# Thirteen wider chunks for fourteen equal ones in the two mixers of a fused attention and mixer kernel

## The chip, the core and the metric

The kernel runs on one core of one Trainium2 chip. The time is device microseconds from launch to end, the median of three runs. TensorE (PE in the rows) multiplies, VectorE (DVE) and ScalarE (ACT) do the elementwise work, GpSimd (POOL) and SyncE (SP) issue most of the transfers.

## The reference

Three blocks follow each other on two samples of 3136 tokens with 256 features: attention whose weights are a squared ReLU, a mixer with a low-rank mix along the tokens, and a mixer with a Fourier transform along tokens and features. Both mixers end in the same feed-forward pair of matmuls with 1024 hidden features.

```python
scores = (1 / S) * z @ z.T
a = u * (np.maximum(scores, 0) ** 2 @ v)             # attention, gated by u

u1 = a + (a.T @ U @ V).T                             # mixer 1: U is 3136x32, V is 32x3136
x = u1 + np.maximum(u1 @ w_ch1, 0) @ w_ch2

u2 = x + np.real(fft(fft(x, axis=1), axis=2))        # mixer 2
un = (u2 - mean(u2)) / np.sqrt(var(u2) + 1e-6)       # over the features
out = u2 + np.maximum(un @ w2_ch1, 0) @ w2_ch2
```

## The kernel before, in words

Everything is kept transposed: features on the 128 partitions (two halves), tokens along the free axis. Each fp32 operand of a large matmul is split into a high part rounded to float32r and a low rest, and a product is made of three float32r matmuls: high by high, high by low, low by high.

The attention runs first, in 14 blocks of 448 queries (7 for each sample). For every pair of key blocks ScalarE makes ReLU and square in a tile of the rotation P (`ptile`, four buffers of 896 columns), VectorE casts it into h and subtracts into l (three buffers each), and TensorE uses h and l two visits later (`LAG = 2`).

The mixers are two layers of 14 chunks of 448 tokens (`CH`), 7 for each sample, none across the border between the samples. One loop (line 1163 on) runs over steps `i`, eight for each chunk, 224 in all. A step issues `hidden(k)` of the present chunk: six matmuls of 448 columns into psH (lines 378 to 380), then ScalarE's ReLU into Hh (line 383) and VectorE's rest into Hl (line 384). Then it issues `project` of the hidden block of two steps before: six matmuls of 448 columns into psC (lines 403 to 405). So Hl of a step has two steps to become ready. In layer 2 the last projection of a chunk is put ahead of the next chunk's first `hidden`, and `finish` follows it at once: two multiplications by rs (line 425), two additions (line 427), two stores.

The order is written out by hand: instructions stand on their engines as the loop issues them, each engine takes its own in that order, and semaphores only hold it back. Beside the two matmul blocks a step advances generators in a list `active`, each to its next `yield`:

- `prep1` (layer 1): a chunk's token mix, two matmuls Gs by Vs of 448 columns (line 268), an addition into x (a P tile), the split into h and l. `Vs` has one buffer and is loaded on GpSimd's queue (line 254).
- `prep2` (layer 2): a chunk's mean and variance, over a row that goes through DRAM (mu, rs) and comes back broadcast; rs has two buffers.
- `fourier(b)`: the transform along 64 and the feature transform of one sample, in 28 advances. `starts` has it begin at step 65 for the first sample and at step 122 for the second. It has to end before the first chunk of layer 2 of its sample is prepared, which the loop asserts.

The list `calm` holds the two `fourier` generators: at a chunk's first step (`k == 0`) they are passed over, so they advance in seven steps of eight. The tables `events`, `folds` and `behind` place the other Fourier pieces (`halves49`: folding, the transform along 49) at given steps. xT is a tile for each sample, 3136 columns wide in each feature half; layer 1 writes its result back into it.

Of the kernel before, what the change touches and what calls it, by code (L numbers as in the profile page):

```python
# [21 lines left out]
CH = 448  # L22
NC = S // CH
NP = 13
# [55 lines left out]
def program(ctx, tc, zT, v, uT, U, V, w1a, w2a, w1b, w2b, b49, f64, fd, rep, mask, out):  # L80
# [25 lines left out]
    def c2(t):  # L106
        return t.rearrange("p (a n) -> p a n", a=2)
# [9 lines left out]
    rs_d = dram.tile([NB * NC, CH], F32, tag="rsd", name="rsd")  # L117
    mu_d = dram.tile([NB * NC, CH], F32, tag="mud", name="mud")
# [38 lines left out]
    def words(raw, np_, n):  # L157
# [5 lines left out]
        e = raw[0:np_, 4 * n : 4 * n + n // 2].bitcast(U16)  # L163
# [82 lines left out]
    class Chunk:  # L246
        def __init__(self, layer, b, c):
            self.layer, self.b, self.c = layer, b, c
            self.sl = slice(c * CH, c * CH + CH)

        def load(self):
            self.vs = com.tile([128, CH + 48], F32R, tag="Vs", name="Vs", bufs=1)[:, 0:CH]
            for k in (0, 64):
                late_dma(out=self.vs[k : k + 64, :], in_=V_d[:, self.sl])
# [4 lines left out]
        def prep1(self):  # L259
            b, vs = self.b, self.vs  # L260
            a = late["xT"][b][:, :, self.sl]
            yield
            if self.c or self.b:
                yield
            x, h, l = c2(ptile()), c2(ctile("h", F32R)), c2(ctile("l", F32R))
            for k in range(2):
                ps = misc()
                mm(ps[:, 0:CH], Gs[b][:, k * 128 : k * 128 + 128], vs, start=True, stop=True)  # L268
                tt(out=x[:, k], in0=ps[:, 0:CH], in1=a[:, k], op=ALU.add)
                hcopy(h[:, k], x[:, k])  # L270
                sub(l[:, k], x[:, k], f(h[:, k]))
                yield
            self.x, self.h, self.l = x, h, l

        def small(self, k):
            if self is not chunks[-1]:
                return late["small"](F32R if k == 2 else F32)
# [4 lines left out]
        def turned(self, s):  # L282
# [3 lines left out]
            q = late["mp"].tile([128, 16], F32, tag="vq", name="vq")[:, 0:14]  # L286
# [3 lines left out]
        def gathered(self, q):  # L290

            vv = late["mp"].tile([32, 64], F32, tag="vv", name="vv")[:, 0:56].rearrange("p (j i) -> p j i", i=4)
# [4 lines left out]
        def spread(self, row_d):  # L297
# [3 lines left out]
            late_dma(out=row_d.rearrange("(p j) -> p j", j=32), in_=turn_back[0:14])  # L301

        def prep2(self):
            b, mp = self.b, late["mp"]
# [3 lines left out]
            pad = late["pad"][:, 0:14]  # L308
            x = late["xT"][b][:, :, self.sl]
            last = self is chunks[-1]  # L310
            nr = b * NC + self.c
# [9 lines left out]
            mu = self.small(2) if last else mp.tile([128, CH], F32, tag="mu", name="mu", bufs=1)  # L321
            late_dma(out=mu, in_=mu_d[nr].partition_broadcast(128))
            for _ in range(1 if last else 3):
                yield
            cc = f(mp.tile([128, 2, CH], F32R, tag="Th", name="Th", bufs=1)) if last else c2(ptile())
            sq = c2(ptile())
# [16 lines left out]
            var, y, r0, ve = (mp.tile([32, 16], F32, tag=t, name=t)[:, 0:14] for t in ("va", "vy", "vr", "ve"))  # L343
# [12 lines left out]
            self.rs = mp.tile([128, CH], F32, tag="rs", name="rs")  # L356
            late_dma(out=self.rs, in_=rs_d[nr].partition_broadcast(128))
# [9 lines left out]
        def split(self, x, y):  # L367
            self.x, self.h, self.l = x, c2(ctile("h", F32R)), c2(ctile("l", F32R))
# [4 lines left out]
        def hidden(self, k):  # L373
            w, mp = late["w"][self.layer][0], late["mp"]
            ps = late["psH"].tile([128, 512], F32, tag="H", name="psH")
# [5 lines left out]
            h = mp.tile([128, CH], F32R, tag="Hh", name="Hh", bufs=3)  # L381
            l = mp.tile([128, CH], F32R, tag="Hl", name="Hl", bufs=3)
            act(out=h, in_=ps[:, 0:CH], func=AF.Relu)  # L383
            stt(out=l, in0=ps[:, 0:CH], scalar=0.0, in1=f(h), op0=ALU.max, op1=ALU.subtract)  # L384
# [3 lines left out]
        def project(self, k):  # L388
# [11 lines left out]
            for a, k, h, l in parts:  # L400
                wh, wl = w.last(k, 0, a), w.last(k, 1, a)
                dst = self.acc[a][:, 0:CH]
# [6 lines left out]
        def finish(self):  # L409
            b = self.b  # L410
            if self.layer == 1:
                for a in range(2):
                    tt(out=late["xT"][b][:, a, self.sl], in0=self.acc[a][:, 0:CH], in1=self.x[:, a], op=ALU.add)
            else:
                o = c2(ptile())
                if self is chunks[-1]:
                    t0, n = self.c * CH, CH // 2
                    for cuts in (((0, 0, CH),), ((1, 0, n), (1, n, CH))):
                        for a, s, e in cuts:
                            tt(out=o[:, a, s:e], in0=self.acc[a][:, s:e], in1=self.x[:, a, s:e], op=ALU.add)  # L420
                            store = nc.scalar.dma_start if a and s == 0 else load
                            store(out=out[b, a * 128 : a * 128 + 128, t0 + s : t0 + e], in_=o[:, a, s:e])
                    return
                for a in range(2):
                    tt(out=o[:, a], in0=self.acc[a][:, 0:CH], in1=self.rs, op=ALU.mult)
                for a in range(2):
                    tt(out=o[:, a], in0=o[:, a], in1=self.x[:, a], op=ALU.add)
                    load(out=out[b, a * 128 : a * 128 + 128, self.sl], in_=o[:, a])

    chunks = [Chunk(y, b, c) for y in (1, 2) for b in range(NB) for c in range(NC)]  # L430


    def attention(stack):
# [83 lines left out]
        def stage():  # L517
            return att.tile([128, 1152], I32, tag="stg", name="stg")
# [730 lines left out]
```

## Time and profile before

| | |
|---|---|
| time, median of 3 runs | 1113.71 us (1113.55 to 1113.74) |
| the profiled execution's own time | 1114.02 us |
| its span, first to last instruction | 1112.2 us |
| attention, until the first step of the mixers | 528.8 us |
| 224 steps of the mixers | 528.8 to 1108.2 us |
| TensorE's granted clock | 1.00 of full speed throughout |
| busy share of PE, DVE, ACT | 100%, 76%, 57% |

Between the span and the execution's own time lie 1.8 us, before the first and after the last instruction. A matmul's recorded duration is its passage through the array, and consecutive matmuls overlap; what one costs TensorE is the distance from its start to the next one's start, which the timeline shows. A line of the timeline that ends in x2 or more stands for so many neighbours, its duration from the first one's start to the last one's end.

### The profile page before, as it was taken

The page shows a single profiled execution, that of the slowest core. Times are in us where ns is not written, and L with a number is a line of the kernel's source. Part 1 is how long each engine was busy: PE and PEld are TensorE (multiplying, and loading weights), DVE is VectorE, ACT ScalarE, POOL GpSimd, SP SyncE. Part 2 cuts the span into 40 slices and gives each one's busy share as a digit, 9 for nine tenths or more (in the row PEclk, how much of TensorE's full clock was granted, in tenths as well). Part 3 has the DMA queues.
Part 4 walks back from the last instruction along what each step waited for, and adds up shares of the span by engine and source line. Part 5 has one row for each costly group of instructions (what it writes and reads, how often), then busy time and mean ns, then how long its engine had stood idle before and what let it go on. Part 6 is the DMA issues. An engine that isn't in the chain of part 4 may idle for free.

```text
span 1112.2 us, 21470 instructions
## 1 busy us (share of the span) xinstructions
PE 1107.0 (100%) x8282; PEld 1060.2 (95%) x8282; DVE 846.5 (76%) x1598; ACT 636.3 (57%) x1101; POOL 189.0 (17%) x313
## 2 busy tenths in 40 slices
PE   9999999999999999999999999999999999999998
PEld 8999999999999999999989999999999999999997
DVE  8877887888788876676667778577678898778863
ACT  8777777878787776675333444343345444435431
POOL 2202221221122102202211112110132111011110
PEclk9999999999999999999999999999999999999999
DMA  5222222424222234211823445331145322121110
GB/s 168 78 57 62 66 77 69 121 72 129 56 71 60 70 100 121 51 34 34 263 70 92 124 153 141 83 78 45 36 98 145 78 66 61 41 59 50 57 44 34
DMA packets 87815, 92.16 MB, mean 83 GB/s; under 512 B 27622, under 2 KB 76506, under 8 KB 87712
## 3 DMA queue, kind: packets, MB, share of 16 engines
q1 hardware_dynamic: 70544, 58.90, 17.8%
q0 software_dynamic: 16816, 31.68, 12.2%
q8 instruction: 65, 1.06, 0.4%
q14 instruction: 38, 0.31, 0.1%
q10 hardware_dynamic: 352, 0.21, 0.1%
HBM read 60.87 MB, written 29.85 MB: 82 GB/s over the span
## 4 chain that ended last, share of the span: by engine, by line
PE 99%; ACT 0%; DMA 0%; DVE 0%; issue 0%; SPq 0%; DVEq 0%; ACTq 0%
PE psO L628 37%; PE psS L586 9%; PE psH L378 8%; PE psC L405 8%; PE psH L380 8%; PE psC L403 8%; PE psH L379 8%; PE psC L404 8%; PE ps_m L1009 0%; DMA zraw<-in_zT 0%; PE ps_g L1009 0%; PE ps_x L1009 0%; PE psS L233 0%; PE ps_g L233 0%; PE ps_x L268 0%; PE ps_m L971 0%
## 5 line engine op out<-in xcount | busy, mean ns | idle before, releaser
L628 PE MATMUL psO<-h,Vt 64*128 64x448 f32 x2744 | 324.0, 359 | 0.2 <-DVE h L597 0.2
L628 PEld LDWEIGHTS psO<-h,Vt 64*128 64x128 f32 x2744 | 280.8, 184 | 3.4 <-DVE h L597 0.9
L383 ACT ACTIVATE Hh<-psH 128x448 fp32r<-128x448 f32 x224 | 121.5, 543 | 241.8 <-PE psH L380 238.6
L93 DVE TENSOR_TENSOR l<-P,h 128x896 fp32r<-128x896 f32 (+2 forms) x237 | 224.8, 954 | 35.4 <-ACT h L90 18.2
L384 DVE SCALAR_TENSOR_TENSOR Hl<-psH,Hh 128x448 fp32r<-128x448 f32 x224 | 138.1, 619 | 107.6 <-ACT Hh L383 105.5
L602 ACT ACTIVATE P<-psS 128x896 f32<-128x896 f32 (+1 forms) x181 | 160.4, 886 | 76.6 <-PE psS L586 74.9
L628 PE MATMUL psO<-l,Vt 64*128 64x448 f32 x1372 | 185.6, 359 | 0.0
L603 ACT ACTIVATE P<-P 128x896 f32<-128x896 f32 (+1 forms) x181 | 167.4, 925 | 5.7
L604 DVE CAST h<-P 128x896 fp32r<-128x896 f32 (+1 forms) x181 | 110.6, 611 | 74.7 <-ACT P L603 73.3
L378 PE MATMUL psH<-h,w 128*128 128x448 f32 x448 | 165.0, 368 | 0.0
L380 PE MATMUL psH<-h,w 128*128 128x448 f32 x448 | 162.4, 362 | 0.0
L405 PE MATMUL psC<-Hh,w 128*128 128x448 f32 x448 | 162.3, 362 | 0.0
L379 PE MATMUL psH<-l,w 128*128 128x448 f32 x448 | 162.2, 362 | 0.0
L404 PE MATMUL psC<-Hl,w 128*128 128x448 f32 x448 | 162.1, 362 | 0.0
L403 PE MATMUL psC<-Hh,w 128*128 128x448 f32 x448 | 162.0, 362 | 0.0
L628 PEld LDWEIGHTS psO<-l,Vt 64*128 64x128 f32 x1372 | 145.6, 184 | 1.1
L586 PE MATMUL psS<-Q,KT 64*128 64x448 f32 x1002 | 132.3, 360 | 0.0
L586 PEld LDWEIGHTS psS<-Q,KT 64*128 64x128 f32 x1002 | 104.1, 184 | 1.7 <-issue 0.4
L378 PEld LDWEIGHTS psH<-h,w 128*128 128x128 f32 x448 | 84.1, 188 | 6.3 <-ACT P L90 0.3
L379 PEld LDWEIGHTS psH<-l,w 128*128 128x128 f32 x448 | 84.2, 188 | 5.8
L404 PEld LDWEIGHTS psC<-Hl,w 128*128 128x128 f32 x448 | 84.0, 187 | 6.0
L403 PEld LDWEIGHTS psC<-Hh,w 128*128 128x128 f32 x448 | 83.9, 187 | 5.7 <-issue 0.2
(287 smaller groups left out, 1149.4 us busy)
## 6 DMA issues: line engine op xcount, KB each, us to landing
out<-P SPq DMA_DIRECT2D x27, 224.0 KB, 1.9
uT<-in_uT SPq DMA_DIRECT2D x13, 448.0 KB, 3.8
aTd<-aT POOLq DMA_DIRECT2D x13, 448.0 KB, 3.0
aNd<-aT POOLq DMA_DIRECT2D x104, 56.0 KB, 2.2
vraw<-in_v SPq DMA_DIRECT2D x18, 256.0 KB, 4.4
scr<-wst SPq DMA_DIRECT2D x16, 256.0 KB, 2.0
Vs<-Vd POOLq DMA_DIRECT2D x28, 112.0 KB, 2.6
xT<-aTd SPq DMA_DIRECT2D x7, 448.0 KB, 4.8
```

The costliest lines, as they stand in the source:

```text
L93: tt(out=o, in0=a, in1=b, op=ALU.subtract)
L378: mm(ps[:, 0:CH], wh, self.h[:, a], start=a == 0, stop=False)
L379: mm(ps[:, 0:CH], wh, self.l[:, a], start=False, stop=False)
L380: mm(ps[:, 0:CH], wl, self.h[:, a], start=False, stop=a == 1)
L384: stt(out=l, in0=ps[:, 0:CH], scalar=0.0, in1=f(h), op0=ALU.max, op1=ALU.subtract)
L403: mm(dst, wh, h, start=k == 0, stop=False)
L404: mm(dst, wh, l, start=False, stop=False)
L405: mm(dst, wl, h, start=False, stop=k == 7)
L586: mm(dst[:, 0:w], k, q[r, kq, o : o + w], start=(kk, kq) == (0, 0), stop=kk == 1)
L602: act(out=A[:, x].rearrange("p (a n) -> p a n", a=2), in_=ps[:, :, 0:w], func=AF.Relu, scale=1.0 / S)
L603: act(out=A[:, x], in_=A[:, x], func=AF.Square)
L628: mm(o[fa][i][:, 0:CH], vt[r, j, k, fa * 128 : fa * 128 + 128], x[r, j * CH : j * CH + CH], start=p == 0 and fa not in [t[1][0] for t in t ...
```

## The change

Both layers take 13 chunks: layer 1 has widths 448, four times 496, eight times 480; layer 2 has twice 512, ten times 480, 448. The seventh chunk of each layer lies across the border between the samples. The loop has 208 steps. A chunk's `parts` lists which of its columns belong to which sample. In layer 1 the border chunk's token mix takes two matmuls in place of one (224 and 256 columns, each with its sample's Gs) and four loads of Vs in place of two; in layer 2 its stores are cut in two.

Wider tiles take more room, so P has three buffers in place of four, rs one in place of two, the conversion scratch `stg` 1024 columns in place of 1152 (the exponent field is kept in the lowest 16 bits of the words themselves), and the last gate of the attention takes its two tiles from h and l in place of P. The two samples' xT become one tile X.

The list `calm` goes, so both `fourier` generators advance in every step. The second starts at step 114 in place of 122, and the `halves49` events are placed at written-out steps.

```diff
+CW = 512
+WIDTHS = {1: [CH] + 4 * [496] + 8 * [480], 2: 2 * [CW] + 10 * [480] + [CH]}
+L1 = len(WIDTHS[1])
...
     def ctile(tag, dt=F32, **k):
-        return com.tile([128, 2 * CH], dt, tag=tag, name=tag, **k)
+        return com.tile([128, 2 * CW], dt, tag=tag, name=tag, **k)
     def ptile():
-        return ctile("P", bufs=4)
+        return ctile("P", bufs=3)
...
     class Chunk:
-        def __init__(self, layer, b, c):
-            self.layer, self.b, self.c = layer, b, c
-            self.sl = slice(c * CH, c * CH + CH)
+        def __init__(self, layer, c):
+            self.layer, self.c, self.n = layer, c, WIDTHS[layer][c]
+            t0 = sum(WIDTHS[layer][:c])
+            t1 = t0 + self.n
+            self.sl = slice(t0, t1)
+            self.parts = [
+                (b, slice(max(t0, b * S) - t0, min(t1, b * S + S) - t0), slice(max(t0, b * S) - b * S, min(t1, b * S + S) - b * S))
+                for b in range(NB)
+                if t0 < b * S + S and t1 > b * S
+            ]
...
             for k in (0, 64):
-                late_dma(out=self.vs[k : k + 64, :], in_=V_d[:, self.sl])
+                for _, here, there in self.parts:
+                    late_dma(out=self.vs[k : k + 64, here], in_=V_d[:, there])
...
                 ps = misc()
-                mm(ps[:, 0:CH], Gs[b][:, k * 128 : k * 128 + 128], vs, start=True, stop=True)
-                tt(out=x[:, k], in0=ps[:, 0:CH], in1=a[:, k], op=ALU.add)
+                for b, here, _ in self.parts:
+                    mm(ps[:, here], Gs[b][:, k * 128 : k * 128 + 128], vs[:, here], start=True, stop=True)
+                tt(out=x[:, k], in0=ps[:, 0:n], in1=a[:, k], op=ALU.add)
...
-            self.rs = mp.tile([128, CH], F32, tag="rs", name="rs")
-            late_dma(out=self.rs, in_=rs_d[nr].partition_broadcast(128))
+            self.rs = mp.tile([128, CW], F32, tag="rs", name="rs", bufs=1)[:, 0:n]
+            late_dma(out=self.rs, in_=rs_d[nr, 0:n].partition_broadcast(128))
...
-                mm(ps[:, 0:CH], wh, self.h[:, a], start=a == 0, stop=False)
-                mm(ps[:, 0:CH], wh, self.l[:, a], start=False, stop=False)
-                mm(ps[:, 0:CH], wl, self.h[:, a], start=False, stop=a == 1)
+                mm(ps, wh, self.h[:, a], start=a == 0, stop=False)
+                mm(ps, wh, self.l[:, a], start=False, stop=False)
+                mm(ps, wl, self.h[:, a], start=False, stop=a == 1)
...
-    xT = late["xT"] = [xpool.tile([128, 2, S], F32, tag=f"xT{b}", name=f"xT{b}") for b in range(NB)]
+    X = late["X"] = xpool.tile([128, 2, NB * S], F32, tag="xT", name="xT")
+    xT = [X[:, :, b * S : b * S + S] for b in range(NB)]
...
-            0: late["gate"], 4: mix1, 1: convert(0), 3: convert(1), 65: fourier(0), 122: fourier(1), 108: weights2(),
+            0: late["gate"], 4: mix1, 1: convert(0), 3: convert(1), 65: fourier(0), 114: fourier(1), 100: weights2(),
         }
-        calm = [starts[65], starts[122]]
-        begin = {8 * n - 8 + (2 if n < 2 * NC else -2): n for n in range(1, len(chunks) - 1)}
+        mix2 = [starts[65], starts[114]]
+        begin = {8 * n - 8 + (2 if n < L1 else -2): n for n in range(1, len(chunks) - 1)}
...
-                at = (b * NC + k) * 8 + 14 if k < 6 else b * NC * 8 + 51 + k
+                at = ((14, 22, 30, 38, 46, 54, 57, 58), (70, 73, 78, 86, 94, 102, 105, 106))[b][k]
...
             for g in list(active):
-                if k == 0 and g in calm:
-                    continue
                 if next(g, "end") == "end":
```

Two places show the new order. The first is TensorE's, in layer 1, at the step where the token mix of the chunk after the sixth begins. Before (ps are banks of PSUM, nh and nl the split input of the transform along 49, Gs the token mix of a sample):

```order
L404 MATMUL psC_8885<-Hl,w 128x448
L405 MATMUL psC_8885<-Hh,w 128x448
L970 MATMUL ps_x<-nh_7820,b49h 128x512
L971 MATMUL ps_x<-nl_7821,b49h 128x512
L972 MATMUL ps_x<-nh_7820,b49l 128x512
L268 MATMUL ps_g<-Vs,Gs_88 128x448
L378 MATMUL psH<-h,w 128x448
L379 MATMUL psH<-l,w 128x448
```

And now, TensorE at the same place:

```order
L415 MATMUL psC_8886<-Hl,w 128x480
L416 MATMUL psC_8886<-Hh,w 128x480
L987 MATMUL ps_x<-nh_7819,b49h 128x512
L988 MATMUL ps_x<-nl_7820,b49h 128x512
L989 MATMUL ps_x<-nh_7819,b49l 128x512
L279 MATMUL ps_g<-Vs,Gs_88 128x224
L279 MATMUL ps_g<-Vs,Gs_89 128x256
L389 MATMUL psH<-h,w 128x480
L390 MATMUL psH<-l,w 128x480
```

Nothing has changed its place there: the matmuls are wider, the mix of the border chunk is cut in two, and the transform along 49 keeps its 512 columns.

The second place is VectorE's, in layer 2 while the second sample's Fourier mixer runs, around the border from one chunk to the next (steps 128 and 129 in both). Hl closes a step; va to vt are the small rows of the statistics, P with psC and rs is `finish`, Tl and the additions into xT are the Fourier mixer's. Before:

```order
L93 TENSOR_TENSOR Tl<-ps_m,Th 128x2x128
L384 SCALAR_TENSOR_TENSOR Hl<-psH,Hh 128x448
L344 TENSOR_REDUCE va<-vv 32x14
L345 TENSOR_SCALAR ve<-va 32x14
L319 TENSOR_REDUCE pad<-vv 32x14
L300 STREAM_TRANSPOSE vt<-pad 32x32
L425 TENSOR_TENSOR P<-psC_11159,rs 128x448
L425 TENSOR_TENSOR P<-psC_11160,rs 128x448
L427 TENSOR_TENSOR P<-P,xT_7804 128x448 x2
L384 SCALAR_TENSOR_TENSOR Hl<-psH,Hh 128x448 x2
```

And now, VectorE at the same steps:

```order
L395 SCALAR_TENSOR_TENSOR Hl<-psH,Hh 128x480
L354 TENSOR_REDUCE va<-vv 32x15
L355 TENSOR_SCALAR ve<-va 32x15
L329 TENSOR_REDUCE pad<-vv 32x15
L311 STREAM_TRANSPOSE vt<-pad 32x32
L96 TENSOR_TENSOR Tl<-ps_x,Th 128x2x128
L1065 TENSOR_TENSOR xT<-xT,A_11451 128x6x32x2
L1065 TENSOR_TENSOR xT<-xT,A_11452 128x6x32x2
L438 TENSOR_TENSOR P<-psC_11289,rs 128x480
L438 TENSOR_TENSOR P<-psC_11290,rs 128x480
L440 TENSOR_TENSOR P<-P,xT 128x480 x2
L395 SCALAR_TENSOR_TENSOR Hl<-psH,Hh 128x480
```

Three rows of the Fourier mixer (Tl and two additions into xT) have moved in between the statistics and `finish`, where the pause kept the step free of them before.

## Rows read from the trace of the kernel before

**Rows 1.** The page: busy time of each engine, share of the span, instructions.
```profile
span 1112.2 us, 21470 instructions
PE 1107.0 (100%) x8282; PEld 1060.2 (95%) x8282; DVE 846.5 (76%) x1598; ACT 636.3 (57%) x1101; POOL 189.0 (17%) x313
```

**Rows 2.** The waits of TensorE: for whom, us in total, times, longest.
```profile
PE psS L756 <- POOL warm L747: 1.0, 1, 1.0
PE psO L628 <- DVE h L597: 0.2, 1, 0.2
```

**Rows 3.** Groups of TensorE by line and shape: busy us, mean ns | idle before.
```profile
L378 PE MATMUL psH<-h,w 128*128 128x448 f32 x448 | 165.0, 368 | 0.0
L268 PE MATMUL ps_x<-Vs,Gs 128*128 128x448 f32 x10 | 3.6, 361 | 0.0
```

**Rows 4.** Timeline of TensorE, one step: start us, us, instruction.
```profile
799.70 0.36 PE L378 MATMUL psH<-h,w 128*128 128x448 f32 x1
...
802.10 0.36 PE L378 MATMUL psH<-h,w 128*128 128x448 f32 x1
```

**Rows 5.** Timeline of TensorE: the feature transform, six matmuls 384 columns wide.
```profile
718.84 0.34 PE L1027 MATMUL ps_m<-Th,fA 128*128 128x384 f32 x1
...
719.88 0.36 PE L378 MATMUL psH<-h,w 128*128 128x448 f32 x1
```

**Rows 6.** Timeline of TensorE: two transforms along 49, three matmuls of 512 columns each.
```profile
635.98 0.39 PE L970 MATMUL ps_m<-nh,b49h 128*128 128x512 f32 x1
...
636.67 0.36 PE L378 MATMUL psH<-h,w 128*128 128x448 f32 x1
...
815.89 0.39 PE L970 MATMUL ps_m<-nh,b49h 128*128 128x512 f32 x1
...
816.59 0.37 PE L378 MATMUL psH<-h,w 128*128 128x448 f32 x1
```

**Rows 7.** Timeline of TensorE: the second Fourier mixer's first matmul along 64.
```profile
859.74 0.37 PE L405 MATMUL psC<-Hh,w 128*128 128x448 f32 x1
860.11 0.68 PE L1009 MATMUL ps_m<-f64s,wr 128*128 128x128 f32 x4
```

**Rows 8.** Timeline of ScalarE and VectorE in the attention: tiles of P.
```profile
207.97 1.09 DVE L93 TENSOR_TENSOR l<-P,h 128x896 fp32r<-128x896 f32 x1
...
211.65 0.93 ACT L602 ACTIVATE P<-psS 128x896 f32<-128x896 f32 x1 [0.96 <-PE psS L586]
```

**Rows 9.** Windows of the mixers: engines' busy us in each, clock, DMA.
```profile
core 0: us, PE busy (x) PEld busy (x) DVE busy (x) ACT busy (x) POOL busy (x), PEclk, DMA share, GB/s
823.80:843.70 19.90, 19.90 (x101) 18.56 (x100) 18.29 (x48) 11.00 (x25) 9.24 (x14) 1.00 0.66 153
843.70:932.90 89.20, 89.20 (x472) 83.57 (x471) 77.51 (x182) 43.96 (x119) 13.47 (x25) 1.00 0.29 76
889.20:911.70 22.50, 22.50 (x125) 21.27 (x123) 20.82 (x50) 11.12 (x30) 4.29 (x8) 1.00 0.35 81
952.10:990.50 38.40, 38.40 (x194) 36.00 (x193) 28.60 (x65) 16.25 (x43) 4.32 (x8) 1.00 0.17 49
```

**Rows 10.** Timeline of VectorE and TensorE around step 23: Hl and its matmul.
```profile
591.49 1.12 DVE L384 SCALAR_TENSOR_TENSOR Hl<-psH,Hh 128x448 fp32r<-128x448 f32 x2
...
592.36 0.36 PE L403 MATMUL psC<-Hh,w 128*128 128x448 f32 x1
```

**Rows 11.** Groups of VectorE by line: busy us, mean ns | idle before.
```profile
L384 DVE SCALAR_TENSOR_TENSOR Hl<-psH,Hh 128x448 fp32r<-128x448 f32 x224 | 138.1, 619 | 107.6 <-ACT Hh L383 105.5
...
L425 DVE TENSOR_TENSOR P<-psC,rs 128x448 f32<-128x448 f32 x26 | 15.2, 603 | 0.8 <-PE psC L405 0.8
...
L427 DVE TENSOR_TENSOR P<-P,xT 128x448 f32<-128x448 f32 x26 | 14.9, 615 | 0.0
...
L1048 DVE TENSOR_TENSOR xT<-xT,A 128x384 f32<-128x384 f32 (+1 forms) x16 | 8.4, 568 | 0.0
...
L93 DVE TENSOR_TENSOR Tl<-ps_m,Th 128x256 fp32r<-128x256 f32 (+1 forms) x10 | 4.0, 401 | 1.8 <-ACT Th L90 1.8
```

More of the change, by code (lines that the diff above doesn't have):

```diff
@@ L276, in small @@
             if self is not chunks[-1]:
-                return late["small"](F32R if k == 2 else F32)
+                return late["small"](F32R if k == 2 else F32)[:, 0 : self.n]
             if k < 2:
@@ L290, in gathered @@
         def gathered(self, q):
-            vv = late["mp"].tile([32, 64], F32, tag="vv", name="vv")[:, 0:56].rearrange("p (j i) -> p j i", i=4)
+            vv = late["mp"].tile([32, 64], F32, tag="vv", name="vv")[:, 0 : self.n // 8].rearrange("p (j i) -> p j i", i=4)
             for i, r in enumerate(quads):
@@ L421, in finish @@
                             store = nc.scalar.dma_start if a and s == 0 else load
-                            store(out=out[b, a * 128 : a * 128 + 128, t0 + s : t0 + e], in_=o[:, a, s:e])
+                            at = slice(there.start + s, there.start + e)
+                            store(out=out[b, a * 128 : a * 128 + 128, at], in_=o[:, a, s:e])
                     return
                 for a in range(2):
-                    tt(out=o[:, a], in0=self.acc[a][:, 0:CH], in1=self.rs, op=ALU.mult)
+                    tt(out=o[:, a], in0=self.acc[a][:, 0:n], in1=self.rs, op=ALU.mult)
                 for a in range(2):
                     tt(out=o[:, a], in0=o[:, a], in1=self.x[:, a], op=ALU.add)
-                    load(out=out[b, a * 128 : a * 128 + 128, self.sl], in_=o[:, a])
-    chunks = [Chunk(y, b, c) for y in (1, 2) for b in range(NB) for c in range(NC)]
+                    for b, here, there in self.parts:
+                        load(out=out[b, a * 128 : a * 128 + 128, there], in_=o[:, a, here])
+    chunks = [Chunk(y, c) for y in (1, 2) for c in range(L1)]
     def attention(stack):
@@ L654, in gate @@
             last = (b, qc) == (1, NC - 1)
-            t, tb = (ptile() if last else att.tile([128, 2 * CH], F32, tag="aT", name="aT") for _ in range(2))
+            if last:
+                t, tb = (f(ctile(x, F32R))[:, 0 : 2 * CH] for x in ("h", "l"))
+            else:
+                t, tb = (att.tile([128, 2 * CH], F32, tag="aT", name="aT") for _ in range(2))
             o, u = acc.pop((b, qc)), uq.pop((b, qc))
@@ L882, in mixer @@
         g = psX.tile([128, 512], F32, tag="g", name="ps_g")[:, 0:D]
-        raw = xT[1].rearrange("p a n -> p (a n)")
-        blocks = [raw[:, s * D : s * D + D] for s in range(24)] + [late["half"]]
+        raw = [xT[1][:, s // 12, s % 12 * D : (s % 12 + 4) * D] for s in range(0, 24, 4)]
+        blocks = [r[:, j * D : j * D + D] for r in raw for j in range(4)] + [late["half"]]
         for s in range(0, 24, 4):
             load(
-                out=raw[:, s * D : (s + 4) * D].rearrange("p (s d) -> p s d", s=4),
+                out=raw[s // 4].rearrange("p (s d) -> p s d", s=4),
                 in_=aN_d[1][128 * s : 128 * s + 512].rearrange("(s p) d -> p s d", p=128),
@@ L1153, in program @@
             for k in range(8):
-                at = (b * NC + k) * 8 + 14 if k < 6 else b * NC * 8 + 51 + k
+                at = ((14, 22, 30, 38, 46, 54, 57, 58), (70, 73, 78, 86, 94, 102, 105, 106))[b][k]
+                ends = [sum(WIDTHS[1][: c + 1]) for c in range(L1)]
+                assert at >= 8 * sum(x < b * S + 392 * (k + 1) for x in ends) + 9
                 go = max(at + 2, 36 + 2 * k)
@@ L1180, in program @@
             if new:
-                assert not (new == 2 * NC and calm[0] in active or new == 3 * NC and calm[1] in active)
+                assert not (new == L1 and mix2[0] in active or chunks[new].parts[-1][0] and new > L1 and mix2[1] in active)
                 norms = [chunks[new].prep(), *norms[:1]]
@@ L1203, in program @@
                 next(last, None)
-            for op, k49 in behind.get(i, []) + folds.get(i, []):
+            for op, k49 in folds.get(i, []):
                 op(k49)
```

81 lines of the change are left out of this document (40 added, 41 removed).

## The prediction

> **What bounds the kernel now.** I read the page's busy times first, then TensorE's waits, then its timeline. TensorE is busy for 1107.0 us of a span of 1112.2 us, VectorE for 846.5 us [rows 1]. Busy alone proves little, since matmuls overlap, so the waits decide: over the whole span TensorE waited twice, 1.0 us at the start and 0.2 us soon after [rows 2]. A stall of a few hundred nanoseconds can still hide in the overlap; the one worth pricing comes below. So the time is the sum of the distances between matmul starts, and a change helps only by making that sum smaller, and hurts if it enlarges it or lets another engine come late.
>
> What does a matmul cost? In a step with nothing beside the chunk's own work, twelve matmuls of 448 columns go from 799.70 to 802.10 [rows 4]: 200.0 ns each. At the granted clock of 1.00 [rows 9], which is the level of 2.4 GHz, 448 columns take 186.7 ns. So 13.3 ns remain. Two widths tell whether these belong to the instruction or to the columns. Six matmuls of 384 columns take 1.04 us from 718.84 to 719.88 [rows 5]: 173.3 ns, against 160.0 for the columns, 13.3 again. Three of 512 columns take 0.69 and 0.70 us [rows 6]: 230 to 233 ns, against 213.3. That is some 2.3 ns more than 13.3 would give, if I take 229 ns, the low end of what two decimals allow. So between 384 and 448 the cost is a fixed 13.3 ns for each instruction plus the columns; somewhere between 448 and 512 a little is added.
>
> **The change, part by part.** *Fewer matmuls.* Each of the six lines of the feed-forward has 448 matmuls [rows 3]: 2688. With 26 chunks of 96 it is 2496. The columns are the same (6272 tokens in each layer), so 192 times 13.3 ns = 2.56 us go.
>
> *Wider matmuls.* Of the 2496, 1728 have 480 columns, 384 have 496, 192 have 512 and 192 keep 448. If 512 columns carry 2.3 ns extra, the 192 of them cost 0.45 us. For 480 and 496 the trace has no row. From below they cost nothing beyond 13.3 ns, as 384 and 448 do; from above they lie on the straight line from 200.0 ns at 448 to 229 at 512, which gives 214.5 for 480 (1.2 above the fixed rule, 2.0 us for 1728) and 221.7 for 496 (1.7 above, 0.7 us for 384). 480 stands as near to the one row as to the other. I take zero for both, because two widths with an exact fixed cost and an excess at the single full-width tile look more like a limit met at 512 than like a slope; the 2.7 us stay in the range.
>
> *The border chunk.* Outside its first chunk layer 1 had 13 chunks with two token-mix matmuls each, 26 (ten of them in rows 3). Now it has 12, of which the border chunk takes two for each: again 26, with the same columns. So this costs nothing, and at most 0.4 us if every cut matmul costs as much as a whole one. The two more loads of Vs and the two more stores stand on GpSimd's and SyncE's queues, whose transfers TensorE has waited for nowhere [rows 2].
>
> *Three buffers for P.* In the attention ScalarE's ReLU takes a P tile that VectorE's subtraction three visits earlier has to have left. At the tightest place that subtraction ends at 209.06 (207.97 and 1.09) and the ReLU starts at 211.65 [rows 8]: 2.6 us of room, so no wait. In layer 2 a chunk takes three P tiles in turn, and the one of `finish` comes round again a chunk later. One buffer for rs makes the next chunk's load wait for `finish` of the present one; in the order it stands some three steps behind that `finish`, and behind it on GpSimd's queue stand the stores and loads of mu, used three advances later. I cost this at nothing; if the cover failed, a chunk's `finish` and not TensorE would be late first.
>
> *No pause in the Fourier mixers.* Their matmuls are the same. What moves is VectorE's work: the second sample's 28 advances now fill steps 114 to 141 instead of being spread over 32. Between 843.70 and 932.90, 32 steps, VectorE was busy 77.51 us of 89.20; in 16 steps without Fourier work (952.10 to 990.50) it was 28.60 of 38.40, that is 1.79 us a step of 2.40 [rows 9]. So the mixer adds 77.51 - 32 x 1.79 = 20.3 us to VectorE and 89.20 - 32 x 2.40 = 12.4 us to TensorE. After the change the base is at most 1.79 x 480/448 = 1.92 us a step of 12 x 213.3 ns = 2.56: 28 x 1.92 + 20.3 = 74 us of VectorE in 28 x 2.56 + 12.4 = 84 us, 88%. Before, two stretches held 92 and 93% (18.29 of 19.90, 20.82 of 22.50) [rows 9] and no wait of TensorE came of it [rows 2]. I cost it at nothing.
>
> *A stall that should go.* The second mixer's first matmul along 64 starts 0.37 us after the matmul ahead of it [rows 7] where 0.20 is normal: it waits 0.17 us for the columns that were fetched three steps earlier. Each of these steps grows by 0.16 us, so this should vanish: -0.17 us; from above 0.
>
> The sum: -2.56 + 0.45 - 0.17 = -2.28 us, plus some hundredths for the cut matmuls: -2.2. The profiled execution took 1114.02 us and would take 1111.8; the median stood 0.31 us below it, so I forecast 1113.71 - 2.2 = **1111.5 us**, 0.20% less. What a measurement of this kernel can tell from no change is about 0.2%, that is 2.2 us: the forecast lies on that line.
>
> **Rivals.** *The cost follows the columns.* On the straight line from 448 to 512 the wider matmuls give back 2.0 + 0.7 + 0.45 = 3.1 us of the 2.56 saved: +0.6 - 0.17, or 1114.1 us. For it speaks that the 512-wide rows are the only ones above 448, against it that 384 and 448 agree in the fixed 13.3 ns [rows 4, 5]. A milder form has half of the 13.3 ns go with the instruction and half with the columns: 1.3 us saved, 1112.4.
>
> The Trainium skill's page "TensorE: Matmul & The Clock Gate", section "Wait — 56ns, not 53.3ns?", gives about 2.5 ns as the fixed cost of a matmul at 2.4 GHz; by that figure only 192 x 2.5 = 0.5 us would go, an estimate of 1113.2 us. The trace disagrees, 13.3 ns at two widths [rows 4, 5], and the measurement decides.
>
> *VectorE comes late, and the kernel is slower.* The place is the border between two chunks of layer 2 under the second Fourier mixer. There one step now holds the statistics' small rows (about 0.7 us), one Tl (0.40), two additions into xT (2 x 0.57), `finish` (2 x 0.60 and 2 x 0.62) and Hl (0.62) [rows 11]: 5.3 us, 5.5 with the wider chunks, against a step of 2.56 us plus about 0.44 of Fourier matmuls; before, the pause left the same step at 3.8. Hl has two steps to become ready, and room was already thin: at step 23 the first of two Hl was ready near 592.05 (half of 1.12 us after 591.49), the matmul of its block stands at 592.36 [rows 10]. Two steps are 0.32 us longer now, and the steps beside the heavy one are light, so I expect the debt to be paid. It decides from the point at which the debt carried into the border exceeds about 1 us. Three borders lie in steps 114 to 141 and three in the first mixer's steps 65 to 92; late by 1 us at each, that is +6 us, or 1111.5 + 6 = 1117.5; at the second mixer's three alone 1114.5.
>
> **How the numbers follow.** The forecast, a fixed cost of 13.3 ns with a small excess, has 0.74, between 1110.7 (no excess at 512, the small stalls gone) and 1112.4 (excess at 496 too). The column rival has 0.18 with 1112.4 to 1114.2, VectorE late has 0.08 with 1114 to 1117.5. The forecast's own range is cut by the line of 0.2% at 1111.48, slightly in favour of faster since its lower half holds the plain rule: 0.42 of its 0.74 are faster, 0.32 the same. The column rival is all the same, of the last one 0.05 is slower and 0.03 the same. Faster 0.42, same 0.53, slower 0.05. To leave out no more than 2 in 10 the range goes from 1110.7 to 1113.6.
>
> **What would show it.** In the changed kernel's timeline twelve matmuls of 480 columns should span 2.56 us (2.57 with the line: 12 x 214.5), so only a stretch of many steps tells: eight clean steps should take 20.48 us against 20.59. The waits of TensorE should still be two rows. VectorE's busy share in the second mixer's stretch should be near 88%, and the Hl before a chunk border should end before its matmul. The first matmul along 64 should follow its predecessor by 0.20 us. The prediction is wrong if 480 columns cost over 214 ns, or if a row of waits or a gap of more than 0.3 us shows at Hl in the borders.

## The result, and the profile after

The changed kernel takes 1124.27 us (median of 4 runs, 1123.4 to 1124.95) against 1113.72 us for the kernel before beside it: a ratio of 1.009, 95% interval 1.0078 to 1.0103. It is 10.5 us slower, where 1111.5 us was forecast. The forecast was wrong, in its sign and in its range. The profiled execution took 1123.9 us.

The page of the changed kernel, to be held against [rows 1]:

```profile
span 1122.1 us, 20996 instructions
...
PE 1115.9 (99%) x8090; PEld 1014.3 (90%) x8090; DVE 845.8 (75%) x1552; ACT 632.9 (56%) x1070; POOL 186.0 (17%) x309
```

TensorE has 192 matmuls fewer, as the change says, and is busy 8.9 us longer. So its matmuls became dearer. VectorE and ScalarE do no more than before.

The waits of TensorE (line waited at and for whom; us in total, times, longest), which answer to [rows 2]:

```profile
PE psC L415 <- DVE Hl L395: 1.1, 1, 1.1
PE psS L772 <- POOL warm L763: 1.0, 1, 1.0
PE psO L641 <- DVE h L610: 0.2, 1, 0.2
```

The last two rows are the old ones. The first is new: a projection waits once for Hl.

What a matmul costs now is read from the timeline of TensorE (start, us, instruction), where [rows 4] showed 200.0 ns for 448 columns. A stretch of eight steps of 480 columns with nothing beside them, then one step of 496 and one of 512:

```profile
970.45 0.38 PE L389 MATMUL psH<-h,w 128*128 128x480 f32 x1
...
991.41 0.38 PE L389 MATMUL psH<-h,w 128*128 128x480 f32 x1
...
577.25 0.39 PE L389 MATMUL psH<-h,w 128*128 128x496 f32 x1
...
579.97 0.39 PE L389 MATMUL psH<-h,w 128*128 128x496 f32 x1
...
835.40 0.39 PE L389 MATMUL psH<-h,w 128*128 128x512 f32 x1
...
838.16 0.39 PE L389 MATMUL psH<-h,w 128*128 128x512 f32 x1
```

The 96 matmuls of 480 columns take 20.96 us, 218.3 ns each, where 20.48 us had been written down as the sign that the forecast holds. The twelve of 496 columns take 2.72 us, 226.7 ns each, almost what 512 columns cost (2.76 us, 230 ns; 229.1 over longer stretches). Beyond the columns' own time and the 13.3 ns these are 5.0, 6.7 and 2.4 ns.

The windows of the mixers (columns as in [rows 9]): the second Fourier mixer's steps 114 to 141, and 16 steps of 480 columns without Fourier work.

```profile
core 0: us, PE busy (x) PEld busy (x) DVE busy (x) ACT busy (x) POOL busy (x), PEclk, DMA share, GB/s
859.40:944.00 84.60, 84.60 (x416) 73.53 (x416) 71.10 (x163) 40.78 (x103) 12.87 (x24) 1.00 0.30 81
970.40:1012.40 42.00, 42.00 (x194) 36.29 (x194) 32.23 (x68) 17.88 (x48) 4.31 (x8) 1.00 0.17 48
```

The granted clock is 1.00 in both, as before, so the dearer matmuls are no matter of the clock. VectorE is busy 71.10 of 84.60 us, 84%, where the forecast had 88%: the stretch that was to become crowded has room.

**The sum of the mixers.** From the first step to the last they took 579.5 us before and 589.1 us after, 9.6 us more. The rows give: fewer matmuls -2.56; 480 columns 1728 x 5.0 ns = +8.6; 496 columns 384 x 6.7 ns = +2.6; 512 columns 192 x 2.4 ns = +0.5; the new stall +1.2 (below); the first matmul along 64 -0.17. That makes +10.2, which is 0.6 us more than was measured; this rest is not attributed.

**The new stall.** The timeline of several engines around it (step 46 of layer 1; the bracket is the idle time before an instruction and who ended it):

```profile
661.24 0.56 SPq L895 DMA_DIRECT2D xT<-aTd  x1
...
662.50 0.16 DVE L941 TENSOR_TENSOR y<-xT 128x8 f32<-128x8 f32 x1
...
666.16 0.63 DVE L941 TENSOR_TENSOR y<-xT 128x192 f32<-128x192 f32 x2 [3.50 <-DMA xT<-aTd]
...
666.58 0.38 PE L414 MATMUL psC<-Hh,w 128*128 128x480 f32 x1
...
667.36 1.19 DVE L395 SCALAR_TENSOR_TENSOR Hl<-psH,Hh 128x480 fp32r<-128x480 f32 x2
...
668.03 0.48 PE L415 MATMUL psC<-Hl,w 128*128 128x480 f32 x1 [1.06 <-DVE Hl L395]
```

VectorE is folding columns of the first sample (line 941) and stops for 3.50 us until a transfer has landed in xT. That transfer (line 895) brings tokens of the second sample, which this fold doesn't read. Behind the fold on VectorE's queue stand two Hl, and TensorE's projection waits for the first: from 666.58 to 668.03 it goes 1.45 us from one matmul to the next, 1.23 more than the 0.22 of a 480-wide one. In the kernel before, at the same step, the same load was issued as shortly ahead of the fold, and the fold went through without a wait:

```profile
649.62 0.47 SPq L878 DMA_DIRECT2D xT<-aTd  x1
...
650.77 0.70 DVE L924 TENSOR_TENSOR y<-xT 128x8 f32<-128x8 f32 x3
```

There the two samples had a tile each; now both lie in one tile X. Not every read of X waits: the fold's first row (128x8) at 662.50 started without one, its two rows of 128x192 did not. Why these and not that one is not shown.

### The profile page after: what moved, and what is told of

Read it like the earlier page. It is cut to its first block, busy times and chain, and to the rows that moved or that the text cites. A ratio compares the mean times of both kernels' runs of the same rounds, so it can differ in the third digit from the quotient of the medians.

```text
span 1122.1 us, 20996 instructions
## 1 busy us (share of the span) xinstructions
PE 1115.9 (99%) x8090; PEld 1014.3 (90%) x8090; DVE 845.8 (75%) x1552; ACT 632.9 (56%) x1070; POOL 186.0 (17%) x309
## 4 chain that ended last, share of the span: by engine, by line
PE 97%; issue 2%; DMA 1%; ACT 0%; DVE 0%; DVEq 0%; SPq 0%; POOL 0%; POOLq 0%
PE psO L641 37%; PE psS L599 9%; PE psC L415 8%; PE psH L389 8%; PE psC L416 8%; PE psC L414 8%; PE psH L391 8%; PE psH L390 8%; PE ps_x L1026 0%; DMA xT<-aTd 0%; PE psS L772 0%; PE ps_m L1026 0%; PE psS L236 0%; PE ps_g L236 0%; PE ps_g L1026 0%
## 5 line engine op out<-in xcount | busy, mean ns | idle before, releaser
L641 PEld LDWEIGHTS psO<-h,Vt 64*128 64x128 f32 x2744 | 272.0, 184 | 9.5 <-DVE h L610 0.7
L394 ACT ACTIVATE Hh<-psH 128x480 fp32r<-128x480 f32 (+3 forms) x208 | 119.1, 573 | 256.6 <-PE psH L391 240.5
L96 DVE TENSOR_TENSOR l<-P,h 128x896 fp32r<-128x896 f32 (+5 forms) x233 | 224.3, 967 | 35.0 <-ACT h L93 17.8
L395 DVE SCALAR_TENSOR_TENSOR Hl<-psH,Hh 128x480 fp32r<-128x480 f32 (+3 forms) x208 | 136.0, 655 | 117.0 <-ACT Hh L394 116.0
L389 PE MATMUL psH<-h,w 128*128 128x480 f32 (+3 forms) x416 | 161.2, 388 | 0.0
L415 PE MATMUL psC<-Hl,w 128*128 128x480 f32 (+3 forms) x416 | 158.6, 381 | 1.1 <-DVE Hl L395 1.1
L416 PE MATMUL psC<-Hh,w 128*128 128x480 f32 (+3 forms) x416 | 158.7, 381 | 0.0
L391 PE MATMUL psH<-h,w 128*128 128x480 f32 (+3 forms) x416 | 158.6, 381 | 0.0
L414 PE MATMUL psC<-Hh,w 128*128 128x480 f32 (+3 forms) x416 | 158.5, 381 | 0.0
L390 PE MATMUL psH<-l,w 128*128 128x480 f32 (+3 forms) x416 | 158.5, 381 | 0.0
L415 PEld LDWEIGHTS psC<-Hl,w 128*128 128x128 f32 x416 | 78.2, 188 | 14.3 <-DVE Hl L395 1.5
L416 PEld LDWEIGHTS psC<-Hh,w 128*128 128x128 f32 x416 | 78.3, 188 | 12.8
L414 PEld LDWEIGHTS psC<-Hh,w 128*128 128x128 f32 x416 | 78.4, 189 | 12.6
## 6 DMA issues: line engine op xcount, KB each, us to landing
nl<-natd SPq DMA_DIRECT2D x16, 196.0 KB
```

The lines of the kernel that those rows point to most:

```text
L96: tt(out=o, in0=a, in1=b, op=ALU.subtract)
L389: mm(ps, wh, self.h[:, a], start=a == 0, stop=False)
L390: mm(ps, wh, self.l[:, a], start=False, stop=False)
L391: mm(ps, wl, self.h[:, a], start=False, stop=a == 1)
L395: stt(out=l, in0=ps, scalar=0.0, in1=f(h), op0=ALU.max, op1=ALU.subtract)
L414: mm(dst, wh, h, start=k == 0, stop=False)
```

## The experiments

### What a matmul costs by its width

The first question was whether the price of 480 columns belongs to the width, or to what runs beside it in this kernel. The kernel before was given a stretch behind its last step in which TensorE runs alone, 48 float32r matmuls of each width, with the feed-forward's weights and an operand that is no longer needed.

```diff
+        mov = com.tile([128, 2 * CH], F32R, tag="h", name="probe")
+        def probe(n, s=0, o=0):
+            for k in range(8):
+                ps = psH.tile([128, 512], F32, tag="H", name="psH")
+                for j in range(6):
+                    yield ps[:, o : o + n], w0.first(k, j % 2, j // 2 % 2), mov[:, s : s + n], j == 0, j == 5
+        for n in (256, 320, 352, 384, 400, 416, 432, 448, 464, 480, 496, 512):
+            for d, w, m, st, sp in probe(n):
+                mm(d, w, m, start=st, stop=sp)
...
+        for d, w, m, st, sp in probe(448, 16):
...
+        for d, w, m, st, sp in probe(448, 32):
...
+        for d, w, m, st, sp in probe(480, 32):
...
+        for d, w, m, st, sp in probe(480, 0, 32):
...
+        for d, w, m, st, sp in probe(512, 16):
...
```

> The kernel before with a probe behind its last step: 48 float32r matmuls each of 256, 320, 352, 384, 400, 416, 432, 448, 464, 480, 496 and 512 columns, alone on the chip's engines, then 448 and 480 with shifted operands, so only TensorE works. Its end is some 160 us later. Theory G (grain): a width that is no multiple of 64 columns costs more than columns / 2.4 GHz + 13.3 ns. It expects 120.0, 146.7, 173.3, 200.0 ns at 256, 320, 384, 448, and at 352, 416 and 480 about 5 ns, at 400, 432, 464 and 496 some 4 to 8 ns more than the formula. Theory L (length): what lies above 448 columns costs more. It expects the formula (160.0, 180.0, 186.7, 193.3 ns) at 352, 400, 416, 432 and an excess only at 464, 480, 496 and 512. Theory C (contention): the excess of 5 ns at 480 comes from what VectorE, ScalarE and transfers do beside it. It expects 213.3 ns at 480 here.

The kernel took 1273.52 us with its probe. A second and a third probe of the same build asked further, with other widths, other starts in the operand, two operand tiles by turns, and one weight block for all 48 in place of the feed-forward's.

```diff
+                    x = alt if two and j % 2 else mov
+                    w = w0.first(0, 0, 0) if same else w0.first(k, j % 2, j // 2 % 2)
```

> The kernel before with a second probe behind its last step, 48 matmuls a case, the engines beside TensorE idle: 448 columns starting at column 64, 128 and 192 of their tile; 416 at 64; 480 at 64, 128, 256; 480 and 512 with two tiles read in turn, as the kernel reads h and l; 480, 512, 448 and 496 with one and the same weight block each time; 512 at 64, 128, 256. Theory P (place): what counts is where the moving operand starts and ends in steps of 64 columns; then 448 at 64, 128 and 192 stays at 200.0 to 200.5 ns (it was 203.8 and 202.1 at 16 and 32), 480 stays near 218 and 512 near 233 at 64, 128 and 256. Theory W (weights): the excess comes from the weight block that is read meanwhile; then one weight block for all gives 213.3 to 214 ns at 480 and 226.7 to 227.5 at 512, and nothing changes with the start. Theory T (two tiles): 512 costs 229 in the kernel and 233 in the first probe because h and l are different tiles; then two tiles in turn give 229 at 512.

```diff
+        for n in (384, 512, 448, 440, 456, 448, 408, 424, 472, 488, 504, 512, 480, 448, 512, 384, 496, 448):
+            for d, w, m, st, sp in probe(n, 0, True):
+                mm(d, w, m, start=st, stop=sp)
```

> The kernel before with a third probe behind its last step, 48 matmuls a case, in this order: 384, 512, 448, 440, 456, 448, 408, 424, 472, 488, 504, 512, 480, 448, 512, 384, 496, 448 columns, all from column 0, two tiles in turn. Theory P: 384 and 448 cost the formula (173.3, 200.0) wherever they stand, all widths between 400 and 512 that are no multiple of 64 cost 1 to 8 ns more; 512 costs 229 or 233. Theory H (history: the excess depends on what ran before): 448 and 512 take other values behind an odd width than behind an even one.

They took 1310.72 and 1294.36 us; each of the three probes is one execution. That TensorE works alone there is shown by a window over the whole first probe (columns as in [rows 9]):

```profile
1110.60:1270.00 159.40, 159.40 (x816) 145.40 (x816) 0.00 (x0) 0.00 (x0) 0.00 (x0) 1.00 0.00 1
```

VectorE, ScalarE and GpSimd are idle, the clock is 1.00, and 816 matmuls have 816 weight loads. A row of the timeline in the second probe is one case, all its 48 matmuls; the distance to the next row's start, over 48, is the price of one:

```profile
1129.85 9.76 PE L1226 MATMUL psH<-probe,w 128*128 128x448 f32 x48
1139.45 9.20 PE L1228 MATMUL psH<-probe,w 128*128 128x416 f32 x48
1148.49 10.64 PE L1230 MATMUL psH<-probe,w 128*128 128x480 f32 x48
1158.96 10.64 PE L1232 MATMUL psH<-probe,w 128*128 128x480 f32 x48
...
1190.40 10.64 PE L1238 MATMUL psH<-probe,w 128*128 128x480 f32 x48
1200.88 10.64 PE L1240 MATMUL psH<-probe,w 128*128 128x480 f32 x48
1211.36 9.76 PE L1242 MATMUL psH<-probe,w 128*128 128x448 f32 x48
...
1230.56 11.16 PE L1246 MATMUL psH<-probe,w 128*128 128x512 f32 x48
1241.56 11.15 PE L1248 MATMUL psH<-probe,w 128*128 128x512 f32 x48
```

For instance 448 columns: (1139.45 - 1129.85) / 48 = 200.0 ns; 416: 188.3; 480: 218.1 to 218.3, also with one weight block (1190.40 to 1200.88); 512: 229.2. In the first and the third probe the timeline merges many widths into one row; there the starts of the single matmuls were read from the trace. All three probes together, with the excess over the columns at 2.4 GHz (the level of a granted clock of 1.00) and the 13.3 ns:

| columns | ns | excess | | columns | ns | excess |
|---|---|---|---|---|---|---|
| 256 | 120.0 | 0 | | 440 | 199.9 | 3.3 |
| 320 | 146.6 | 0 | | 448 | 200.1 | 0.1 |
| 352 | 160.1 | 0.1 | | 456 | 207.6 | 4.2 |
| 384 | 173.4 | 0 | | 464 | 210.0 | 3.4 |
| 400 | 180.0 | 0 | | 472 | 210.9 | 0.9 |
| 408 | 186.6 | 3.3 | | 480 | 218.3 | 5.0 |
| 416 | 188.2 | 1.5 | | 488 | 219.9 | 3.2 |
| 424 | 193.4 | 3.4 | | 496 | 226.6 | 6.6 |
| 432 | 196.0 | 2.7 | | 504 | 228.8 | 5.4 |
| | | | | 512 | 229.0 | 2.3 |

What follows:

- 480 and 496 columns cost the same with every other engine idle as in the mixers. So contention with other engines (theory C) is out.
- The excess follows neither a straight line nor a limit met at 512. It is nil up to 400 and at 448, small at 472, and between 1.5 and 6.6 ns at the other widths tried from 408 on. 440 columns cost as much as 448. Theory L fails at 416 and 432, theory G at 352 and 400.
- It makes no difference whether the weight block changes, or whether one or two operand tiles are read: in the second probe 480 stayed at 218.3 ns with one weight block, with two operand tiles, and with both; 448 (200.0) and 512 (228.9) did not move either. Every matmul had a weight load of its own in all these cases, so whether the load itself has a part was not tested.
- For 448 columns, what ran just before has no part: they took 200.0 to 200.4 ns in all four places of the third probe, behind different widths.
- The start in the operand matters, as the rows below show. 448 columns from column 16 on took 204.0 ns, from 32 on 202.1; from 128 and 192 on 200.0 in the second probe, where 480 from 64, 128 and 256 on stayed at 218.2 to 218.3. A start 32 columns in lowered 480 to 215.8, so the excess hangs on the columns that are read, not on the count alone. Moving the output by 32 columns did nothing (218.1).
- 512 columns took 233.3 ns in the first probe, from column 0 and from 16 alike, and 228.8 to 229.1 in both later ones, with one operand tile or two, so two tiles (theory T) are not the reason. Both prices come up again within one execution of a whole kernel (the one with widths 448 and 512 below). What sets them is open.
- A theory that only multiples of 64 columns are free of excess falls with 400 (none) and 472 (0.9). Which rule gives these numbers stays open.

The first probe's timeline of TensorE: 448 columns from column 16 on, 448 from 32, 480 from 32, 480 with its output from column 32.

```profile
1218.64 9.95 PE L1221 MATMUL psH<-probe,w 128*128 128x448 f32 x48
1228.43 9.87 PE L1223 MATMUL psH<-probe,w 128*128 128x448 f32 x48
1238.13 10.53 PE L1225 MATMUL psH<-probe,w 128*128 128x480 f32 x48
1248.49 10.63 PE L1227 MATMUL psH<-probe,w 128*128 128x480 f32 x48
```

### Width alone, in the whole kernel

A probe prices a matmul, not a kernel. Two runs change the widths alone, each against a run beside it that is otherwise the same. To keep the stall out, all of these move the load at its root one step: `fetches` is the table of steps at which blocks of the second sample are loaded.

```diff
-        fetches.update((at, (1, k, k + 1)) for k, at in enumerate((26, 29, 33, 44, 46, 51, 53)))
+        fetches.update((at, (1, k, k + 1)) for k, at in enumerate((26, 29, 33, 44, 47, 51, 53)))
```

First this edit by itself, in the changed kernel:

> The changed kernel with one load of the second sample's tokens issued at step 47 in place of step 46, behind the fold of the first sample's tokens at step 46. Theory M (one merged tile): that fold waits 3.5 us for a load whose columns it does not read, because both samples now lie in one tile, and TensorE is held 1.3 us by it; expected 1.3 us less than the changed kernel, 1123.0 us against 1124.3. Rival: the wait moves to the next fold or the delay had another cause; 1124.3 us.

Measured: 1122.5 us (1122.07 to 1122.63), ratio to before 1.0074 (1.0059 to 1.0089). The waits of TensorE are the two old rows again:

```profile
PE psS L772 <- POOL warm L763: 1.0, 1, 1.0
PE psO L641 <- DVE h L610: 0.2, 1, 0.2
```

So the stall was worth 1.8 us by the medians and 1.3 us between the mixers of the two profiled executions, and it went with the load. The rest, 8.2 us above before (1114.3 us beside this run), is not the stall.

With this edit kept, still 13 chunks in each layer, but only widths 448 and 512:

```diff
-WIDTHS = {1: [CH] + 4 * [496] + 8 * [480], 2: 2 * [CW] + 10 * [480] + [CH]}
+WIDTHS = {1: [CH] + 7 * [CW] + 5 * [CH], 2: 2 * [CW] + 5 * [CH, CW] + [CH]}
```

> As e2, but each layer takes 13 chunks of 512 (seven) and 448 (six) columns; the number of matmuls is that of the changed kernel. Theory W (the widths 480 and 496 cost it all): a matmul of 512 columns takes 229.2 ns, one of 448 takes 200.0 ns, so the feed-forward takes 2 x 96 x (7 x 229.2 + 6 x 200.0) = 538.4 us against 537.6 before; expected 1114.2 to 1114.6 us. Theory S (the smaller buffers, the cut chunk or the Fourier mixer without pauses cost several us): 1117 us or more.

Measured: 1114.54 us (1113.96 to 1116.09), ratio 1.0005 (0.9996 to 1.0014). The same number of matmuls, the same columns, a border chunk as well, the same buffers, and 8.0 us less than with 480 and 496. The sum comes near: 192 x 13.3 ns saved are 2.56 us, 1344 matmuls of 512 columns at 2.4 ns excess cost 3.2, the first matmul along 64 gives back 0.17, in all +0.5 us; measured +0.2.

The timeline of its profiled execution (1115.6 us, the second slowest of the ten) shows two prices for 512 columns. Below are four steps in layer 1, the two matmuls of the cut token mix (128 and 384 columns, merged into one row), and four steps in layer 2:

```profile
591.60 0.40 PE L389 MATMUL psH<-h,w 128*128 128x512 f32 x1
...
602.80 0.40 PE L389 MATMUL psH<-h,w 128*128 128x512 f32 x1
...
656.24 0.45 PE L279 MATMUL ps_g<-Vs,Gs 128*128 128x128 f32 x2
...
1032.89 0.39 PE L389 MATMUL psH<-h,w 128*128 128x512 f32 x1
...
1043.87 0.39 PE L389 MATMUL psH<-h,w 128*128 128x512 f32 x1
```

48 matmuls take 11.20 us in the first stretch (233.3 ns each) and 10.98 in the second (228.8). The dear price held from 572 us on until the two matmuls at 656.24; behind them the cheap one held to the end. So the width alone does not fix the price of 512 columns; what switches it was not tested. 362 matmuls at 4.5 ns make 1.6 us of this execution. With them the sum gives +2.1 us, where its mixers (581.3 us) took 1.9 more than those of before.

The other way round: 14 chunks, so that the number of matmuls is that of before, with the twelve inner chunks of each layer 480 and 416 columns wide in turn. Besides the widths shown here and the load, the step numbers of the Fourier pieces are those of before, as in the 14-chunk runs of the next section.

```diff
-WIDTHS = {1: [CH] + 4 * [496] + 8 * [480], 2: 2 * [CW] + 10 * [480] + [CH]}
+WIDTHS = {y: [CH] + 6 * [CH + 32, CH - 32] + [CH] for y in (1, 2)}
```

> As e7, still 14 chunks and 2688 matmuls a kernel, but the twelve inner chunks of each layer are 480 and 416 columns in turn, so that number of matmuls and columns are those of e7. Theory P (a width between multiples of 64 costs more): by the probes 480 costs 218.3 ns and 416 188.2 ns, that is 5.0 and 1.5 ns over columns / 2.4 GHz + 13.3 ns; 2 x 6 x 96 x (5.0 + 1.5) = 7.5 us more than e7, about 1121.7 us. Rival (the excess belongs to 13 chunks, not to the width): as e7, 1114.3 us.

Measured: 1121.92 us (1121.52 to 1122.22), ratio 1.0068 (1.0051 to 1.0085). Its timeline of TensorE, four steps of 480 columns and four of 416:

```profile
1004.85 0.35 PE L416 MATMUL psC<-Hh,w 128*128 128x416 f32 x1
...
1013.89 0.35 PE L416 MATMUL psC<-Hh,w 128*128 128x416 f32 x1
...
1023.84 0.38 PE L389 MATMUL psH<-h,w 128*128 128x480 f32 x1
...
1034.32 0.38 PE L389 MATMUL psH<-h,w 128*128 128x480 f32 x1
```

48 matmuls take 9.04 us at 416 (188.3 ns) and 10.48 at 480 (218.3 ns). A pair costs 406.6 ns where two of 448 cost 400.0 for the same 896 columns: 1152 pairs x 6.6 ns = 7.6 us. Measured were 7.6 us more than before and 7.7 more than the same kernel with 14 chunks of 448 (1114.25 us, next section). No wait beyond the two old ones shows. So the widths alone make the kernel this much slower.

### The rest of the change without the widths

All of the change but the widths (and so without a border chunk): 14 chunks of 448, the one tile X, three P buffers, one rs, the smaller `stg`, no pause, and before's step numbers.

```diff
-WIDTHS = {1: [CH] + 4 * [496] + 8 * [480], 2: 2 * [CW] + 10 * [480] + [CH]}
+WIDTHS = {1: 14 * [CH], 2: 14 * [CH]}
...
-            0: late["gate"], 4: mix1, 1: convert(0), 3: convert(1), 65: fourier(0), 114: fourier(1), 100: weights2(),
+            0: late["gate"], 4: mix1, 1: convert(0), 3: convert(1), 65: fourier(0), 122: fourier(1), 108: weights2(),
...
-                at = ((14, 22, 30, 38, 46, 54, 57, 58), (70, 73, 78, 86, 94, 102, 105, 106))[b][k]
+                at = (b * NC + k) * 8 + 14 if k < 6 else b * NC * 8 + 51 + k
```

> The changed kernel with 14 chunks of 448 columns in each layer and the step numbers of the kernel before for the second Fourier mixer and the tables; it keeps the three buffers of P, the one of rs, the merged tile of both samples and the Fourier mixers without a pause. Theory W (widths): 1113.7 us, and up to 1.3 us more if the fold at step 46 again waits for a load that it does not need: 1113.7 to 1115.0. Theory S (one of the other parts costs several us): 1117 us or more.

Measured: 1116.25 us (1115.2 to 1118.4), ratio 1.002 (1.001 to 1.0029), 1.25 us over the upper end that theory W gave and below the 1117 of theory S. Its waits of TensorE and the fold on VectorE:

```profile
PE psC L415 <- DVE Hl L395: 0.8, 1, 0.8
PE ps_m L1026 <- DMA wr<-scr: 0.3, 1, 0.3
...
653.52 0.63 DVE L941 TENSOR_TENSOR y<-xT 128x192 f32<-128x192 f32 x2 [2.46 <-DMA xT<-aTd]
```

It is the same stall, with matmuls of the old width and steps of the old length: the wide chunks didn't make it. With the load moved from step 46 to 47 as above:

> As e4 (the changed kernel with 14 chunks of 448), with the load of the second sample's tokens at step 47 in place of 46. Theory M (the fold at step 46 waits for a load it does not need): the row of TensorE waiting 0.8 us for Hl goes, and 1.0 us with it: about 1 us less than e4, that is about 1 us above the kernel before, of which some 0.3 us is the wait of the first matmul along 64. Rival: the wait moves to the fold at step 54, and e4 and this one take the same.

Measured: 1114.25 us (1113.9 to 1114.8), ratio 1.0001 (0.9992 to 1.0011). The fold no longer waits:

```profile
651.23 0.70 DVE L941 TENSOR_TENSOR y<-xT 128x8 f32<-128x8 f32 x3
```

So fewer P and rs buffers, no pause and the shared tile together cost nothing that can be measured, apart from that one transfer. It is worth 2.0 us here by the medians and 1.1 us between the mixers of the two profiled executions; about 1 us had been expected.

The pause by itself, taken out of the kernel before:

```diff
-                if k == 0 and g in calm:
-                    continue
```

> The kernel before, only the pause of the Fourier mixers at a chunk's first step taken out; 14 chunks of 448 columns, all tiles as before. Theory F (the pause hides nothing): no change, within 0.5 us of the kernel before. Theory V (VectorE comes late at a chunk border without the pause): TensorE waits for Hl about 1 us at several of the six borders, 2 to 6 us more, with rows of waits for Hl.

Measured: 1113.91 us (1113.56 to 1114.4), ratio 0.9999 (0.999 to 1.0008), waits as in [rows 2]. The pause neither gains nor costs anything that can be measured.

## Why the prediction was wrong

**What bounds the kernel: right.** TensorE's starts set the time before and after. The lost microseconds are distances between starts, and one wait.

**Fewer matmuls, -2.56 us: right, and not enough.** 13.3 ns is the fixed part at every width from 256 to 400 and at 448. With widths that carry little more (448 and 512) thirteen chunks came out 0.2 us from fourteen, by the sum of this saving and the excess at 512, as far as it was measured.

**Wider matmuls, +0.45 us: this step failed.** The forecast put 480 and 496 columns at zero excess and gave them 2.7 us in the range, by a straight line between 448 and 512. Measured were 5.0 ns for each of 1728 and 6.7 for each of 384, that is 8.6 and 2.6 us. The upper end was no bound: it assumed that the excess between two known widths lies between theirs, 0 and 2.3 ns. 480 columns cost 218.3 ns against 214.5 on the line, 496 cost 226.7 against 221.7; that 480 columns cost over 214 ns was one of the signs named for a wrong forecast. Both known neighbours happened to be cheap widths. The three widths in [rows 4 to 6] could not tell that the excess jumps about. What could be said beforehand is what an error costs: each ns of excess at 480 columns is 1728 x 1 ns = 1.7 us, more than half of the saving.

**The rival "the cost follows the columns"** had the right place and the wrong size: +0.6 us, where the widths cost +11.7 against -2.56 saved. The Trainium skill's page "TensorE: Matmul & The Clock Gate", section "Wait — 56ns, not 53.3ns?", gives about 2.5 ns as fixed cost; the probe does not agree for these matmuls, 13.3 ns remain at each of six widths from 256 to 448 columns.

**The border chunk, three P buffers, one rs, no pause: right at nothing.** For the buffers and the pause the 14-chunk run with the load moved and the run without the pause show it. These have no border chunk; the run with widths 448 and 512 has one, and lands 0.2 us from before with everything in it. In the changed kernel the cut token mix takes 104.5 and 123 ns, 227 in place of 218, twice: hundredths in all.

**VectorE late at the borders: didn't come.** Its share was 84%. By the trace every Hl of steps 114 to 141 was ready at least 1.8 us ahead of its first matmul, and every one of steps 65 to 92 at least 2.9 us. The room that the prediction saw at step 23 was read one matmul too early: line 403 reads Hh, and the first matmul to read that Hl started at 592.55, 0.5 us behind it. The one late Hl, of step 47, belongs to the stall, which has another cause.

**The stall at the first matmul along 64: right.** The matmul follows at 0.23 us, the usual distance of a 512-wide one, where [rows 7] had 0.37. With steps of the old width it stayed: the two 14-chunk runs wait 0.3 and 0.2 us there.

```profile
870.67 0.39 PE L416 MATMUL psC<-Hh,w 128*128 128x512 f32 x1
870.90 0.61 PE L1026 MATMUL ps_x<-f64s,wr 128*128 128x128 f32 x4
```

**The one tile X: left out.** The sum has no term for it, though the change names it. In the trace the first sample's folds have to wait for a load's transfer at five steps (14, 30, 38, 46, 54), at one before; at one of the five, step 46, the transfer lands too late. That cost 1.8 us by the medians and 1.3 us by the profiled executions of the run that moves the load. That the shared tile is the reason is argued from the fold without a wait in the kernel before; no run parts the tile alone.

## What to carry to other kernels

Before a tile's width is changed, time that width: the price need not lie on the line between two measured ones, and 2000 matmuls turn 5 ns into 10 us. When two buffers become one, walk the reads of the one half past the writes of the other in the order of instructions, since a read may now wait for a transfer that it doesn't use. Where an engine is bound by a sum of many equal parts, the first experiment is the part alone, over a range of sizes.

## What the runs showed of the hardware that was not expected

- Beyond the columns' own time, the distance between float32r matmuls with 128 x 128 weights does not rise steadily with the width: 400 columns (180.0 ns) and 448 (200.1 ns) carry the fixed 13.3 ns alone, 408 (186.6), 456 (207.6), 480 (218.3) and 496 (226.6) carry 3 to 7 ns more. No rule was found.
- 512 columns have two prices, 228.8 and 233.3 ns, and one execution showed each of them over a long stretch.
- Per column 448 costs 0.4464 ns, 472 0.4467, 512 0.447, 400 0.450, 480 0.455, 496 0.457. So the kernel before already has the cheapest width of those tried, and no kernel run here is faster than it.
- A moving operand that starts 16 columns into its tile made 448 columns 3.9 ns dearer, 32 columns in 2.0 ns dearer, while 128 or 192 columns in changed nothing.
